# A hand-ordered plan for retention attention and a SoLU layer on one core: small column work in pairs, half states copied on three engines, eight chunks with the plain output weight, and a new order of all steps

## The chip, the cores and the metric

The kernel runs on one core of one Trainium2 chip. The metric is the device time of one execution in microseconds (us). Beside the plain runs there is one profiled execution, whose trace gives the start and the length of every instruction on TensorE (PE, with its weight loads as PEld), VectorE (DVE), ScalarE (ACT), GpSimd (POOL) and of every transfer that SyncE (SP) issues. Times inside the trace are counted from its first instruction.

## The reference, cut to what matters

Eight sequences of 576 rows pass through retention with eight heads of 64 columns; the joined heads (512 columns) pass through a wide layer with a softmax gate and a layer norm, and through an output weight.

```python
# q, k, v: (8, 8, 576, 64); w_in: (512, 1024); w_out: (1024, 512); g_ln: (1024,); all float32
gamma = 1.0 - 2.0 ** (-5.0 - np.arange(H))
Dmat = np.where(rel >= 0, gamma[:, None, None] ** rel[None], 0.0)   # rel = row - column
ret = (q @ k.transpose(0, 1, 3, 2) / np.sqrt(64)) * Dmat @ v
x = ret.transpose(0, 2, 1, 3).reshape(8 * 576, 512)
h = x @ w_in
e = np.exp(h - h.max(-1, keepdims=True))
solu = h * e / (e.sum(-1, keepdims=True) + 1e-9)
mu = solu.mean(-1, keepdims=True)
var = ((solu - mu) ** 2).mean(-1, keepdims=True)
out = ((solu - mu) / np.sqrt(var + 1e-6) * g_ln) @ w_out
```

## The kernel before, in words

**Chunks.** Each sequence has four chunks of 128 rows and a tail of 64; the tails of two sequences share one chunk. That makes 36 chunks. Two sequences alternate, so chunks 0, 2, 4 and 6 are the first sequence, 1, 3, 5 and 7 the second, and 8 their common tail; then the next two sequences follow. Retention is done chunk by chunk: scores inside the chunk, and a running state (one 64 by 64 block for each head) that carries all earlier chunks of the sequence.

**One chunk, step by step.** `lq`, `lk`, `lv` (lines 151 to 160) load the rows of q, k and v, 256 KB each, into rings of eight buffers. `q`, `k`, `v` (lines 171 to 180) cast them to 16 bits, q and v with a factor for each row and head. `TL:a.b` (line 188) is one group of transposes on TensorE: q and k of chunk a, and the gated rows u of an older chunk b; `eX` and `eY` (lines 224 to 229) copy its two halves out of PSUM. `sc` (line 234) makes the scores, `m0` (line 255) multiplies the decay mask in, `kp` (line 266) makes the chunk's part of the state, `t` (line 308) adds it to the old state, `s16` (line 318) makes the 16-bit copy of the new state, as two instructions for the two halves of the partitions, and `s32` (line 325) the decayed float copy. `xs` and `xv` (lines 278 and 294) add what the old state and the chunk itself give to the same PSUM bank, `xT` (line 333) copies the sum out. `mm1` (line 351) is the product with w_in, 16 matmuls of 512 columns; `max`, `exp`, `solu`, `sq` (lines 369, 379, 408 and 427) are the row maximum, the exponential with its row sum, the gate product with its row sum, and the sum of squared deviations. `w1`, `w2` and `pow` (lines 401, 434 and 441) make the row's factor from these sums, one column of 128 values at a time. `mm2` (line 479) is the product with the output weight, `osb` (line 498) multiplies the row factor while copying out of PSUM, `st` (line 509) stores 128 rows of the result.

**The output weight.** The mean over the 1024 gated columns must be taken out. Two ways are used. For chunks below `RAW`, 5 before, `uc` (line 415) subtracts the mean from the gated rows, and `mm2` uses `w_raw16`, the weight times g_ln, which `ws` (line 543) makes. For the other chunks the mean is taken out of the weight: `mean` (line 558) is a matmul of ones with `w_raw16`, `evm` copies its result out, and `cw` (line 570) subtracts it, eight blocks into `w_out16`. So `mean` needs all eight `ws`, and these need the four loads `wo` of w_out. In the same way the first `mm1` needs the four loads `wi` of w_in and the casts `cwA` and `cwB`.

**The order.** Nothing is scheduled by a planner at run time. `PLAN` (lines 584 to 681) is one list of words, followed from left to right (`follow`, line 684): `name:chunk@engine/banks`, with v for VectorE, s for ScalarE and g for GpSimd. Each engine does its own steps in the order of the list, and so does SP's queue of transfers, where loads and stores stand in one row. A step that waits holds up all later steps of its engine. `warm:k` (line 577) is k matmuls on zeros whose result nobody reads. The order of the transfers in the old list is:

```
wi:0 lk:0 lq:0 lq:1 lk:1 wi:1 lv:0 wi:2 wi:3 lv:1 lq:3 lk:3 lq:2 lk:2 lv:3 lv:2 lq:4 lk:4 lq:5 lk:5 lk:6
lv:4 lv:5 lq:6 lv:6 wo:2 wo:0 wo:3 wo:1 lq:7 lq:8 lk:7 lk:8 lv:7 lq:9 lk:9 lq:10 lk:10 st:0 lv:8 lv:9
lq:11 st:1 lv:10 lk:11 lv:11 st:3 lq:12 lk:13 lv:13 lq:13 lk:12 lq:15 lq:14 lk:14 lk:15 lv:12 lv:15 st:2
lk:17 st:4 lq:17 st:7 lk:19 st:5 lv:17 lv:16 lk:16 lv:14 st:6 lq:16 lv:18 lv:19 st:8 lq:18 st:9 st:10 lk:18
lq:19 lq:22 lq:20 st:11 lv:23 lv:21 lv:20 lk:21 lq:26 lk:20 lq:21 lq:24 lk:22 lk:26 st:12 lv:26 lq:23 lk:23
lk:24 lq:25 lv:22 st:14 st:13 lk:27 lv:28 lk:25 st:15 lv:27 lq:27 lq:28 lv:24 lv:25 st:16 lq:35 lk:29 lk:28
lq:29 st:18 st:17 lv:30 lk:30 lv:29 lk:32 st:19 lk:34 lq:30 lk:33 lk:35 lq:32 st:20 st:22 lv:34 lq:31 lk:31
lq:33 st:21 lv:35 lq:34 lv:31 lv:33 lv:32 st:25 st:24 st:23 st:26 st:27 st:28 ...
```

## Time and profile before

| what | value |
|---|---|
| three runs | 220.24, 222.17 and 223.47 us, median 222.17 us |
| the profiled execution, its own time | 222.2 us |
| its span, first to last instruction | 220.5 us |
| TensorE clock granted, mean | 0.994 |
| moved by DMA | 42.51 MB, 193 GB/s over the span |
| read from and written to HBM | 32.53 MB and 9.44 MB |

The profile's page gives busy time for each engine, the same in forty slices, the transfers, and groups of like instructions with their count, mean length and the idle time before them. The share of a whole span hides that the start, the middle and the end have different limits, so the prediction goes by stretches of time. The lost time that it speaks of is, at a point of the trace, the time on the clock less the time that TensorE had spent on work that the result needs; `warm` matmuls count as lost.

### The profile page before, as it was taken

How to read it: one execution, taken by the hardware profiler on the slowest of the kernel's cores; microseconds unless marked ns; L12 is line 12 of the kernel's file. 1: busy time of each engine (PE TensorE's matmuls, PEld its weight loads, DVE VectorE, ACT ScalarE, POOL GpSimd, SP SyncE). 2: the span in 40 equal slices, each digit the busy share in tenths (PEclk: the TensorE clock that was granted, in tenths of full speed). 3: DMA queues.
4: the chain of work that ended last, by engine and by line, in shares of the span. 5: the costliest groups of instructions: out<-in, count | busy, mean ns of one | idle time of the engine just before them, and what ended most of it. 6: DMA issues, size and time to landing. Idle time of an engine off the chain costs nothing. (4 is left out here: it accounts for less than half of the span.)

```text
span 220.5 us, 8347 instructions
## 1 busy us (share of the span) xinstructions
PE 203.5 (92%) x3486; PEld 122.2 (55%) x3486; DVE 192.2 (87%) x316; ACT 169.3 (77%) x273; POOL 160.5 (73%) x270
## 2 busy tenths in 40 slices
...
DMA  6999999997999989999998997899889920310224
GB/s 160 264 310 195 225 205 299 253 204 166 205 262 190 187 234 250 239 281 222 201 226 204 251 253 170 206 240 221 183 209 212 193 103 0 98 52 4 95 98 143
DMA packets 120806, 42.51 MB, mean 193 GB/s; under 512 B 114496, under 2 KB 114752, under 8 KB 120768
## 3 DMA queue, kind: packets, MB, share of 16 engines
q1 hardware_dynamic: 119728, 41.98, 82.8%
...
q14 instruction: 11, 0.09, 0.2%
HBM read 32.53 MB, written 9.44 MB: 190 GB/s over the span
## 5 line engine op out<-in xcount | busy, mean ns | idle before, releaser
L341 PE MATMUL ps<-w_in,xT 128*64 128x512 f16 x576 | 68.3, 381 | 0.3 <-DVE tt L132 0.2
L341 PE MATMUL ps<-w_out,tt 128*64 128x512 f16 x480 | 56.3, 380 | 0.0
L409 DVE SCALAR_TENSOR_TENSOR u<-ps,e 128x1024 f16<-128x1024 f32 (+1 forms) x37 | 43.7, 1188 | 4.2 <-ACT e L380 3.8
L370 DVE TENSOR_REDUCE col_nm<-ps 128x1 f32<-128x1024 f32 (+1 forms) x37 | 43.9, 1188 | 3.9 <-PE ps L341 3.2
L380 ACT ACTIVATE e<-ps,col_nm 128x1024 f32<-128x1024 f32 (+1 forms) x37 | 40.5, 1096 | 8.1 <-DVE col_nm L370 7.2
L130 ACT COPY tt<-ps 128x1024 f16<-128x1024 f16 (+1 forms) x46 | 42.4, 960 | 5.1 <-PE ps L207 4.4
L247 DVE TENSOR_TENSOR ret<-ps,masks 128x1024 f16<-128x1024 f32 x36 | 43.5, 1216 | 2.9 <-PE ps L240 1.9
L341 PEld LDWEIGHTS <-xT 128*64 128x64 f16 x576 | 31.1, 110 | 25.8 <-ACT xT L130 1.0
L341 PEld LDWEIGHTS <-tt 128*64 128x64 f16 x560 | 31.1, 110 | 24.0 <-issue 0.4
L428 ACT ACTIVATE e<-u,col_su 128x1024 f32<-128x1024 f16 (+1 forms) x37 | 41.8, 1132 | 1.6 <-DVE u L409 1.6
L166 POOL TENSOR_TENSOR q<-qf,small 128x512 f16<-128x512 f32 x33 | 34.5, 1049 | 1.7 <-DMA qf<-in_q_dram 1.4
L166 POOL TENSOR_TENSOR v<-vf,small 128x512 f16<-128x512 f32 x31 | 32.8, 1061 | 2.0 <-DMA vf<-in_v_dram 1.8
L130 ACT CAST xT<-ps 128x512 f16<-128x512 f32 x33 | 19.3, 585 | 12.1 <-PE ps L300 8.8
L322 POOL CAST s<-t 64x256 f16<-64x256 f32 x64 | 26.6, 416 | 2.2 <-DVE col_nmu L416 0.2
L442 POOL TENSOR_TENSOR col_rs<-col_w,mhalf 128x1 f32<-128x1 f32 x36 | 21.2, 592 | 8.2 <-DVE col_w L435 7.9
L506 ACT ACTIVATE o_sb<-ps,col_rs 128x512 f32<-128x512 f32 x30 | 20.5, 691 | 6.2 <-POOL col_rs L442 5.0
L132 POOL CAST k<-kf 128x512 f16<-128x512 f32 x30 | 19.1, 642 | 7.9 <-DMA kf<-in_k_dram 7.6
L132 DVE COPY tt<-ps 128x1024 f16<-128x1024 f16 (+1 forms) x32 | 19.4, 615 | 3.5 <-PE ps L207 3.5
L579 PE MATMUL ps<-zeros 128*128 128x512 f16 x62 | 18.1, 428 | 1.2 <-DVE zeros L698 1.2
L402 POOL TENSOR_SCALAR col_w<-col_s 128x1 f32<-128x1 f32 x36 | 11.0, 309 | 10.6 <-ACT e L380 10.2
L327 POOL TENSOR_TENSOR s<-t,small 128x256 f32<-128x256 f32 x24 | 14.8, 618 | 4.8 <-DVE t L313 4.1
L207 PE MATMUL ps<-ident,q 64*128 64x64 f16 x288 | 11.0, 191 | 6.4 <-DVE u L409 2.1
...
## 6 DMA issues: line engine op xcount, KB each, us to landing
kf<-in_k_dram SPq DMA_DIRECT2D x32, 256.0 KB, 5.1
qf<-in_q_dram SPq DMA_DIRECT2D x32, 256.0 KB, 5.2
vf<-in_v_dram SPq DMA_DIRECT2D x32, 256.0 KB, 4.9
out_dram<-o_sb SPq DMA_DIRECT2D x32, 256.0 KB, 3.4
w_in<-in_moe_w_in_dram SPq DMA_DIRECT2D x4, 512.0 KB, 5.6
w_out<-in_moe_w_out_dram SPq DMA_DIRECT2D x4, 512.0 KB, 7.0
...
```

The costliest lines, as they stand in the source:

```text
L130: nc.scalar.copy(out=out, in_=in_)
L132: {"v": nc.vector, "g": nc.gpsimd}[eng].tensor_copy(out=out, in_=in_)
L166: {"v": nc.vector, "g": nc.gpsimd}[eng].tensor_tensor(out=out, in0=in_, in1=table.unsqueeze(2).to_broadcast([P, H, D]), op=ALU.mult)
L247: nc.vector.tensor_tensor(out=ret[n % RB][:, 4 * e : 4 * e + w].rearrange("p a b -> p (a b)"), in0=bank(b0, w * P), in1=masks[:, 1 if is_t ...
L322: nc.gpsimd.tensor_copy(out=st16[b % 2][c % 2][ee, :, e], in_=T_OF[n][ee])
L341: nc.tensor.matmul(out=o[ee], lhsT=lhs(ee), rhs=rhs, start=start, stop=stop)
L370: nc.vector.tensor_reduce(out=col("nm", n, j), in_=h(n, j), axis=AX.X, op=ALU.max, negate=True)
L380: nc.scalar.activation(out=e_[n % EB][:, part(j)], in_=h(n, j), func=ACT.Exp, bias=col("nm", n), accum_out=col("s", n, j),)
L409: nc.vector.scalar_tensor_tensor(out=u_[n % UB][:, part(j)], in0=h(n, j), scalar=1.0, in1=e_[n % EB][:, part(j)], op0=ALU.mult, op1=ALU.mu ...
L428: nc.scalar.activation(out=e_[n % EB][:, part(j)], in_=u_[n % UB][:, part(j)], func=ACT.Square, bias=col("su", n), scale=-1.0 * DFF, accum ...
L442: nc.gpsimd.tensor_tensor(out=col("rs", n), in0=col("w2", n), in1=mhalf, op=ALU.pow)
L506: nc.scalar.activation(out=dst, in_=o, func=ACT.Copy, scale=col("rs", n))
```

## The change

The change leaves the arithmetic as it is, apart from what runs where and when.

- `w1`, `w2` and `pow` handle the columns of two chunks, 2k and 2k+1, in one instruction (`pair`), 19 times each where there were 36; only chunks 34 and 35 are done alone. `w1` moves from GpSimd to VectorE. The row factor of the first chunk of a pair is now there only when the sums of the second are.
- `s16` is one half of the partitions at a time, each with its own engine: 26 halves on GpSimd, 24 on ScalarE, 14 on VectorE, where GpSimd did all 64.
- `RAW` is 8, so eight chunks go through `uc` and `w_raw16`, and `w_out16` is first needed by chunk 9. Of the eight `uc` steps five are on GpSimd and three on VectorE (five on VectorE before); of the eight `cw` steps five are on GpSimd, as two instructions each, and three on VectorE (all on VectorE before).
- `PLAN` is a new order of all steps. Some casts and copies change engines in it: `k` has 23 on GpSimd, 12 on ScalarE and 1 on VectorE (30, 6 and 0 before), `v` 35 on GpSimd and 1 on VectorE (31 and 5). `warm` has 57 matmuls (62 before). The other steps have the same number as before.
- The new names `ut_` and `dT` are not used: the ring has length 0 and the plan holds no `dT`.

The order of the transfers in the new list, to its end:

```
lq:0 lk:1 wi:0 lv:0 lk:0 lq:2 lq:1 lv:1 wi:3 lk:2 wi:1 wi:2 lq:4 lk:3 lv:2 lq:5 lq:3 lv:4 lk:4 lk:5 lv:3
lk:6 wo:3 lq:6 wo:2 wo:0 lv:5 wo:1 lv:6 lk:7 lq:7 lv:7 lq:9 lq:8 lk:8 lk:9 lq:10 lk:11 lv:8 lk:14 lk:10
lq:11 lv:9 lv:10 st:0 st:3 lq:12 st:1 lq:13 lk:12 lv:13 lk:13 lv:11 st:2 lq:14 lv:15 lv:12 lq:15 lk:17 st:6
st:4 lk:15 st:5 lq:16 lk:16 st:7 lv:14 lv:19 lq:17 lv:16 lk:20 lk:18 lq:19 st:9 st:8 lv:17 lk:19 lq:18 lv:18
lv:20 lk:23 lq:20 lk:22 lk:21 lq:22 lq:25 st:10 lv:21 lq:21 lk:26 st:11 lq:23 lk:25 st:14 lv:22 lq:24 lk:24
lq:27 st:12 lv:24 st:15 lq:26 lk:27 st:13 lk:29 lv:23 lv:29 lk:28 lk:33 st:16 lq:30 lq:29 lv:25 st:17 lq:35
lv:28 st:18 lv:27 st:19 lk:30 lk:35 lv:26 lq:28 lq:32 st:20 lk:31 lv:32 lq:31 lv:31 lv:33 st:21 lq:34 lv:30
lq:33 st:23 lk:32 lk:34 st:22 lv:35 lv:34 st:26 st:27 st:25 st:24 st:29 st:28 ...
```

The diff, with the plan cut to the start and the places that the prediction speaks of:

```diff
--- before.py
+++ after.py
@@ -75,7 +75,7 @@
         return chunks[n][1] == 4
 
 
-    LB, QB, KB, TB, RB, XB, EB, UB, UCB, OB, TQ = 8, 4, 6, 5, 3, 3, 3, 3, 2, 4, 2
+    LB, QB, KB, TB, RB, XB, EB, UB, UCB, OB, TQ, UTB = 8, 4, 6, 5, 3, 3, 3, 3, 2, 4, 2, 0
 
     def ring(count, shape, dtype, name):
         return [const.tile([P] + shape, dtype, name=f"{name}{i}") for i in range(count)]
@@ -86,7 +86,7 @@
     ident = const.tile([P, P], F16, name="ident")
     ones = const.tile([P, P], F16, name="ones")
     zeros = const.tile([P, 512], F16, name="zeros")
-    mhalf = const.tile([P, 1], FP, name="mhalf")
+    mhalf = const.tile([P, 2], FP, name="mhalf")
     gln = const.tile([P, NF], FP, name="gln")
     g32 = const.tile([P, NF], FP, name="g32")
     w_in32 = const.tile([P, 4, DFF], FP, name="w_in32")
@@ -107,6 +107,7 @@
     e_ = ring(EB, [DFF], FP, "e")
     u_ = ring(UB, [DFF], F16, "u")
     uc_ = ring(UCB, [DFF], F16, "uc")
+    ut_ = ring(UTB, [8, P], F16, "ut")
     o_sb = ring(OB, [DM], FP, "o_sb")
     cols = {}
 
@@ -317,9 +318,8 @@
     @step
     def s16(n, j, eng, bk):
         (b,), c = chunks[n]
-        for e in range(2):
-            ee = slice(64 * e, 64 * e + 64)
-            nc.gpsimd.tensor_copy(out=st16[b % 2][c % 2][ee, :, e], in_=T_OF[n][ee])
+        ee = slice(64 * j, 64 * j + 64)
+        copy(eng, st16[b % 2][c % 2][ee, :, j], T_OF[n][ee])
 
     @step
     def s32(n, j, eng, bk):
@@ -397,10 +397,15 @@
     def ssadd(n, j, eng, bk):
         add(nc.vector, "ss", n)
 
+
+    def pair(name, n):
+        return cols[name][:, n : n + (2 if n < NCH - 2 else 1)]
+
     @step
     def w1(n, j, eng, bk):
-        nc.gpsimd.tensor_scalar(
-            out=col("w1", n), in0=col("s", n), scalar1=col("s", n), scalar2=1e-6 * DFF,
+        col("w1", n)
+        nc.vector.scalar_tensor_tensor(
+            out=pair("w1", n), in0=pair("s", n), scalar=1e-6 * DFF, in1=pair("s", n),
             op0=ALU.mult, op1=ALU.mult,
         )
 
@@ -413,6 +418,16 @@
 
     @step
     def uc(n, j, eng, bk):
+        if eng == "g":
+            nc.gpsimd.tensor_scalar(
+                out=col("nmu", n), in0=col("su", n), scalar1=-1.0 / DFF, scalar2=0.0, op0=ALU.mult,
+                op1=ALU.add,
+            )
+            nc.gpsimd.tensor_scalar(
+                out=uc_[n % UCB], in0=u_[n % UB], scalar1=1.0, scalar2=col("nmu", n), op0=ALU.mult,
+                op1=ALU.add,
+            )
+            return
         nc.vector.tensor_scalar(
             out=col("nmu", n), in0=col("su", n), scalar1=-1.0 / DFF, scalar2=None, op0=ALU.mult,
             op1=ALU.bypass,
@@ -432,14 +447,19 @@
 
     @step
     def w2(n, j, eng, bk):
+        col("w2", n)
         nc.vector.scalar_tensor_tensor(
-            out=col("w2", n), in0=col("ss", n), scalar=1.0 / DFF**2, in1=col("w1", n),
+            out=pair("w2", n), in0=pair("ss", n), scalar=1.0 / DFF**2, in1=pair("w1", n),
             op0=ALU.mult, op1=ALU.add,
         )
 
     @step
     def pow_(n, j, eng, bk):
-        nc.gpsimd.tensor_tensor(out=col("rs", n), in0=col("w2", n), in1=mhalf, op=ALU.pow)
+        col("rs", n)
+        w = pair("w2", n)
+        nc.gpsimd.tensor_tensor(
+            out=pair("rs", n), in0=w, in1=mhalf[:, 0 : w.shape[1]], op=ALU.pow
+        )
 
     def lp_src(n, c):
         return u_[n % UB][:, c * P : (c + 1) * P]
@@ -480,14 +500,25 @@
         WHERE["o", n, j] = bk[0]
         w = DM if j is None else DM // 2
         a = 0 if j is None else j * w
-        t = tt[TL_OF["u", n]]
-        t = t if j is not None else t[:, 8:16]
+        if n in DT:
+            t = ut_[DT.index(n) % UTB]
+        else:
+            t = tt[TL_OF["u", n]]
+            t = t if j is not None else t[:, 8:16]
         wt = w_raw16 if n < RAW else w_out16
         for c in range(NF):
             wide_mm(
                 bank(bk[0], w), lambda m: t[:, c, m], wt[:, c, a : a + w],
                 c == 0, c == NF - 1,
             )
+
+
+    DT = []
+
+    @step
+    def dT(n, j, eng, bk):
+        src = uc_[n % UCB] if n < RAW else u_[n % UB]
+        nc.sync.dma_start(out=ut_[DT.index(n) % UTB], in_=src, transpose=True)
 
     def o_part(n, j):
         w = DM if j is None else DM // 2
@@ -568,6 +599,12 @@
 
     @step
     def cw(c, j, eng, bk):
+        if eng == "g":
+            w = w_out32[:, c]
+            gc = g32[:, c : c + 1].to_broadcast([P, DM])
+            nc.gpsimd.tensor_tensor(out=w, in0=w, in1=gc, op=ALU.mult)
+            nc.gpsimd.tensor_tensor(out=w_out16[:, c], in0=w, in1=mean_sb, op=ALU.subtract)
+            return
         nc.vector.scalar_tensor_tensor(
             out=w_out16[:, c], in0=w_out32[:, c], scalar=g32[:, c : c + 1], in1=mean_sb,
             op0=ALU.mult, op1=ALU.subtract,
@@ -582,104 +619,107 @@
 
 
     PLAN = """
...
+        lq:0 warm:30/7 lk:1 wi:0 lv:0 lk:0 lq:2 lq:1 k:1@g lv:1 wi:3 v:0@v q:0@v lk:2 k:0@v
+        TL:0./140 wi:1 kp:0/5 eY:0.@s warm:3/7 t:0 eX:0.@v wi:2 sc:0/01 q:1@v warm:2/7 q:2@v
+        TL:1./261 warm:5/7 lq:4 eY:1.@s v:1@g m0:0 eX:1.@s cwA:0@g s16:0.0@v lk:3 sc:1/01
+        s16:0.1@g kp:1/4 m0:1 warm:4/7 lv:2 k:2@s t:1 xv:1/6 cwB:3@s cwB:0@v TL:2./352 s32:1
+        xT:1@s warm:2/7 lq:5 cwA:1@v cwA:3@g s16:1.0@s xv:0/6 eX:2.@s warm:2/7 eY:2.@v cwB:1@g
+        sc:2/34 warm:2/7 lq:3 cwA:2@v cwB:2@s m0:2 mm1:1/01 lv:4 q:4@g xT:0@v lk:4 k:3@s
+        mm1:0/56 max:1 s16:1.1@s lk:5 v:2@g exp:1 xs:2/4 max:0 s32:0 xv:2/4 lv:3 warm:3/7
+        xT:2@s g32 q:5@g solu:1 exp:0 mm1:2/23 lk:6 q:3@g sq:1 solu:0 wo:3 v:4@g TL:3./713
+        warm:3/0 eX:3.@s eY:3.@v lq:6 uc:0@g max:2 k:4@s xs:3/4 sc:3/01 sq:0 kp:2/6 wo:2 m0:3
+        k:5@g TL:4.0/754 exp:2 uc:1@g t:2 wo:0 eX:4.0@v eY:4.0@s v:3@g solu:2 TL:5.1/160 lv:5
+        warm:1/0 eX:5.1@s s32:2 xv:3/4 eY:5.1@v sc:4/23 uc:2@g xT:3@s wo:1 kp:3/7 m0:4 sc:5/01
+        ws:7@s mm1:3/45 k:6@s lv:6 q:6@g t:3 s16:2.1@s m0:5 s16:3.0@s s16:2.0@s s32:3 ws:6@s
+        lk:7 xs:4/3 max:3 kp:4/7 ws:4@g xv:4/3 ws:5@s TL:6.2/601 xT:4@s t:4 lq:7 ws:1@g exp:3
+        eX:6.2@v mm1:4/23 ws:0@v s32:4 lv:7 eY:6.2@s solu:3 v:5@g s16:4.0@s sc:6/67 s16:3.1@s
+        lq:9 ws:3@g s16:4.1@v ws:2@s xv:5/5 max:4 xs:6/4 xs:5/5 kp:5/0 xT:5@s mean/1 lq:8
+        v:6@g m0:6 exp:4 uc:3@g lk:8 w1:0 w1:2 k:7@s t:5 xv:6/4 solu:4 kp:6/7 evm mm1:5/56
+        lk:9 q:7@g xT:6@s sq:3 uc:4@v lq:10 v:7@g t:6 TL:7.3/432 sq:2 mm1:6/01 eX:7.3@v
...
+        lq:18 m0:16 eY:17.13@s mm1:15/34 s16:14.0@g lv:18 s32:14 xT:14@s lv:20 s16:14.1@v
+        v:17@g t:15 sq:12 t:16 lk:23 sc:17/67 max:15 v:19@g lq:20 mm1:14/12 s16:16.0@s
+        s16:15.0@s m0:17 lk:22 exp:15 q:18@g xv:16/0 xs:16/0 max:14 mm2:10/5 k:19@g s16:16.1@s
+        lk:21 xT:16@s v:18@g s16:15.1@s solu:15 exp:14 lq:22 xs:17/6 xv:17/6 kp:19/7 w1:10
+        kp:18/0 xT:17@s TL:19.15/344 t:19 lq:25 k:23@g t:18 sq:15 mm1:16/67 solu:14 eX:19.15@s
...
+        s16:21.0@g lk:33 s16:21.1@v exp:21 m0:22 mm1:20/34 osb:16@s solu:21 eX:23.19@s v:23@g
...
+        s16:24.0@s osb:20@s st:20 xv:27/7 q:28@g max:25 sc:26/56 lk:31 xs:26/4 mm2:21/3 lv:32
+        v:26@g m0:26 lq:31 exp:25 lv:31 w1:22 lv:33 xv:26/4 solu:25 TL:28.24/263 xT:26@s
...
+        osb:33@s st:34 mm2:35.0/6 st:33 osb:35.1@s st:35.1 osb:35.0@v st:35.0
     """
-    RAW = 5
+    RAW = 8
```

169 lines of the change are left out of this document (73 added, 96 removed).

## The prediction

> **What bounds the kernel now.** I read the page first: the shares of the engines, and the slices of the transfers.
>
> ```profile
> span 220.5 us, 8347 instructions
> PE 203.5 (92%) x3486; PEld 122.2 (55%) x3486; DVE 192.2 (87%) x316; ACT 169.3 (77%) x273; POOL 160.5 (73%) x270
> ...
> DMA  6999999997999989999998997899889920310224
> ...
> q1 hardware_dynamic: 119728, 41.98, 82.8%
> ...
> kf<-in_k_dram SPq DMA_DIRECT2D x32, 256.0 KB, 5.1
> ...
> w_in<-in_moe_w_in_dram SPq DMA_DIRECT2D x4, 512.0 KB, 5.6
> ```
>
> PE leads, but the transfers are at 8 or 9 tenths in nearly every slice until about 175 us. Then the windows; the second fence is the same table for the `warm` line alone.
>
> ```profile
> 10.00:40.00 30.00, 27.52 (x449) 14.71 (x451) 24.89 (x39) 19.28 (x32) 24.26 (x36) 1.00 1.08 254
> 40.00:70.00 30.00, 27.70 (x480) 16.81 (x478) 29.17 (x42) 25.36 (x39) 27.93 (x39) 1.00 0.97 204
> 70.00:103.50 33.50, 32.81 (x613) 20.49 (x609) 31.53 (x51) 29.73 (x47) 30.93 (x55) 1.00 1.02 237
> 103.50:129.70 26.20, 24.53 (x520) 15.65 (x516) 23.33 (x35) 23.59 (x37) 20.25 (x31) 1.00 1.04 222
> 129.70:160.00 30.30, 27.41 (x491) 17.06 (x492) 26.64 (x42) 22.40 (x38) 23.79 (x42) 1.00 0.92 211
> 160.00:203.80 43.80, 43.20 (x764) 27.29 (x758) 42.14 (x64) 36.91 (x61) 28.44 (x54) 1.00 0.45 109
> ```
>
> ```profile
> 10.00:40.00 30.00, 9.64 (x35) 2.60 (x35) 1.00 1.08 254
> ```
>
> The first number after each length is PE's busy time. PE loses 30 - 27.52 + 9.64 = 12.1 us from 10 to 40, then 2.3, 0.7, 1.7, 2.9 and 0.6 us. DVE is at 97% from 40 to 70 and the limit there. From 103 to 160 no engine is: 4.6 us go although DVE has 6.5 idle. The waits of that stretch (108 to 160) and the casts that end them tell why.
>
> ```profile
> POOL k L132 <- DMA kf<-in_k_dram: 6.7, 4, 3.5
> ...
> ACT k L130 <- DMA kf<-in_k_dram: 2.6, 1, 2.6
> ```
>
> ```profile
> 19.70 0.61 POOL L132 CAST k<-kf 128x512 f16<-128x512 f32 x1 [0.60 <-DMA kf<-in_k_dram]
> ...
> 70.16 1.05 POOL L166 TENSOR_TENSOR q<-qf,small 128x512 f16<-128x512 f32 x1 [0.59 <-DMA qf<-in_q_dram]
> ...
> 110.62 0.61 POOL L132 CAST k<-kf 128x512 f16<-128x512 f32 x1 [3.45 <-DMA kf<-in_k_dram]
> ...
> 132.91 0.61 POOL L132 CAST k<-kf 128x512 f16<-128x512 f32 x1 [1.42 <-DMA kf<-in_k_dram]
> ...
> 154.61 0.62 ACT L130 CAST k<-kf 128x512 f16<-128x512 f32 x1 [2.61 <-DMA kf<-in_k_dram]
> ```
>
> By the order of the list these are `k:3`, `q:13`, `k:21`, `k:25` and `k:32`. I count the queue in units of 256 KB: a load or store of 128 rows is one, the two halves of a joined tail together one, a `wi` or `wo` two. Their places are units 16, 59, 94, 112 and 129, so one unit takes 1.23, 1.19, 1.18, 1.19 and 1.20 us, counted from the start of the trace. The queue runs as one straight line of 1.19 us a unit, whatever the engines do. It is the second limit beside PE, and each cast in the list has an earliest time: its unit times 1.19.
>
> **The change, part by part.** First the engines, with these groups.
>
> ```profile
> L322 POOL CAST s<-t 64x256 f16<-64x256 f32 x64 | 26.6, 416 | 2.2 <-DVE col_nmu L416 0.2
> ...
> L442 POOL TENSOR_TENSOR col_rs<-col_w,mhalf 128x1 f32<-128x1 f32 x36 | 21.2, 592 | 8.2 <-DVE col_w L435 7.9
> ...
> L402 POOL TENSOR_SCALAR col_w<-col_s 128x1 f32<-128x1 f32 x36 | 11.0, 309 | 10.6 <-ACT e L380 10.2
> ...
> L435 DVE SCALAR_TENSOR_TENSOR col_w<-col_ss,col_w 128x1 f32<-128x1 f32 x36 | 8.3, 241 | 0.3
> ...
> L571 DVE SCALAR_TENSOR_TENSOR w_out<-w_out,g,mean_sb 128x512 f16<-128x512 f32 x8 | 7.0, 908 | 0.0
> ...
> L420 DVE TENSOR_SCALAR uc<-u,col_nmu 128x1024 f16<-128x1024 f16 x5 | 4.2, 833 | 0.2
> ...
> L130 ACT COPY tt_last<-ps 128x256 f16<-128x256 f16 x2 | 0.8, 400 | 0.0
> ...
> L132 DVE COPY tt_last<-ps 128x256 f16<-128x256 f16 x2 | 0.6, 278 | 0.0
> ```
>
> POOL loses 38 halves at 0.416 (15.8 us), 17 `pow` at 0.592 (10.1) and all 36 `w1` at 0.309 (11.1): -37.0. It gains ten `cw` instructions of the shape of its q cast, 1.05 each (10.5); five `uc`, each a column at 0.31 and 1024 elements at between two casts (1.2) and two products (2.1), say 1.4, as it has one tensor in (8.6); net four `v` and minus seven `k` (about 0). Net about -18 of 160. DVE loses five `cw` (4.5), 17 `w2` (4.1), two `uc` (1.7) and four `v`; it gains 19 `w1` at `w2`'s 0.241 (4.6) and 14 halves. A half on DVE or ACT has no row; nearest are the copies of 256 columns, 0.28 and 0.40. From below the 0.24 of one column bounds both; from above, a DVE instruction between two SBUF tiles can stretch, as `uc` did:
>
> ```profile
> L420 DVE TENSOR_SCALAR uc<-u,col_nmu x5: 497/642/1351, 27.0 to 49.6; 128x1024 f16<-128x1024 f16 x5
> ```
>
> So up to 0.28 + 0.85. I take the copies, which have the same 256 columns: +3.9 on DVE (3.4 to 15.8), 24 x 0.40 = 9.6 on ACT (5.8 to 9.6), which also gets six `k` at 0.62 (3.7). DVE comes out some 4 down, ACT some 12 up to 181 of 220. None of this is on PE's path outside 40 to 70, where DVE is relieved (the first `w_out16` product is chunk 9's now, so `cw` is due later as well); ACT's additions are covered by its 51 us of idle time, and without that each half costs its 0.40.
>
> The pair adds a wait: `osb` of an even chunk now waits for `sq` of the next. The list puts both `sq` ahead of each `pow`, so I cost it at nothing; behind it stand the store and, in SP's queue, the loads after that store (a rival below). `k:3` on ACT waits for unit 18, 21.4 us; `exp:1` behind it needs the maximum of the first `mm1`, due at about 22.7, so that wait is covered. PE's work is unchanged; five `warm` fewer only make room.
>
> Then the moved loads, which decide. For PE's work left after a step I use the chain of waits.
>
> ```profile
> 190.50 1.85 PE ps L341 x16
> ...
> 192.80 0.12 PE ps L270 x8
> ...
> 193.58 0.47 PE ps L207 x32
> ...
> 195.89 0.22 PE ps L300 x8
> 196.12 0.33 PE ps L240 x8
> ...
> 204.81 0.57 PE ps L207 x32
> ...
> 210.16 0.23 PE ps L455 x16
> ```
>
> A wide product is 1.85, `kp` 0.12, `xv` and `xs` 0.22, `sc` 0.33, half a `TL` 0.25; the whole list (70 wide products, four halves, the mean at 1.9, 36 `sc`, 64 `xv` and `xs`, 32 `kp`, 71 halves of `TL`) comes to 183. Four gates of the new order, each at its unit times 1.19:
>
> Start: `wi:2` is unit 16 (19.0 us; `wi:3` was unit 13), so the first `mm1` slips by nearly 4 us, but two then run in a row. The mean needs `wo:1`, unit 36 (42.8) and a `ws` of 1.05: 43.9 us, with 17.2 us of useful PE work before it, so 26.7 lost. Before it began here:
>
> ```profile
> 45.15 1.92 PE L341 MATMUL ps<-w_raw,ones 128*64 128x512 f16 x16
> ```
>
> with 21.2 of work done, 24.0 lost. The start is 2.7 worse. `kp:18` needs `lv:18`, unit 87 (103.5) and the cast 1.05: 104.6, then 43 wide products (79.6), four halves (3.8), 18 `sc`, 32 `xv` and `xs`, 15 `kp`, 39 halves of `TL`, `lp`: 108.1. `xv:23` needs unit 114 (135.7): 136.8, then 76.4. `xv:26` is the last: `lq:28`, unit 131 (29 + 28 + 27 full loads, 18 stores, 26 half units, 16 for the weights), lands at 155.9, and on POOL `v:26` stands behind `q:28`: two casts of 1.05, so 158.1. After it come 22 wide products (40.7), four halves (3.8), 8 `sc` (2.6), 16 `xv` and `xs` (3.5), 8 `kp` (1.0), 19 halves of `TL` (4.8), `lp` 0.2: 56.6. PE's end to the span's end, the last `osb` and store, was 4.8. Gates in us of span: 217.5, 218.0, and 158.1 + 56.6 + 4.8 = 219.5.
>
> The same sum for the old list: `kp:31` waits for `v:31`, which POOL casts at 175.05:
>
> ```profile
> 175.05 1.04 POOL L166 TENSOR_TENSOR v<-vf,small 128x512 f16<-128x512 f32 x1
> ...
> 213.80 1.91 PE L341 MATMUL ps<-w_out,tt_last 128*64 128x256 f16 x32
> ```
>
> 176.1 + 38.7 + 4.8 = 219.6 against the 220.5 measured. So the method is 0.9 short, and I add 0.6 to the new 219.5 (there is less after its gate to go wrong on DVE): span 220.1. What the start loses and what DVE saves from 40 to 70 both vanish in this gate. The profiled execution's own time, 222.2, is 1.7 over its span and equal to the median of 222.17; so 220.1 gives 221.8.
>
> A rule speaks against the line of 1.19. The Trainium skill, "DMA: Bandwidth & Descriptors", section "Why small descriptors are slow (HBM only)", gives a 256-byte descriptor 11 cycles where 8 carry data; with the 435 GB/s that this page's section "Where 436 GB/s comes from" states, that is 316 GB/s, an estimate of 0.83 us a unit, and unit 131 would land at 109 us. The trace has 1.19, so the measurement decides; by the page no load would be a gate, which is the first rival.
>
> **The rivals.** (1) The loads are no gate: the straight line was the engines' pace and not the queue's. For it: DMA's share reaches 1.08 in the windows, so 1.0 need not be full. Against it: the line holds at 19.7 us as at 154.6. Then there remain the start's 26.7 lost and, with DVE relieved, some 0.8 of the old 2.3 from 40 to 70: 183 + 27.5 + 4.8 = 215.3 of span, 217.0.
>
> (2) Slower: SP's queue stands at stores. `st:0` to `st:8` stand close behind their `osb`, and every load behind a store waits with it.
>
> ```profile
> SPq L513 <- ACT o_sb L506: 37.4, 14, 10.7
> ```
>
> It decides where SP stands longer than a transfer is under way (5.1 us, the `kf` row): only then does the line bend. Two such stands of 3 us beyond that, ahead of `lq:28`, give 226.1 of span, 227.8. Against it: these waits have not bent the line before.
>
> (3) Also slower: the three `uc` on POOL in the first 35 us, and the casts behind them, cost 2.1 each or more, and POOL, not the loads, is late at `q:28`. It decides when POOL is over 155.9 there; 116 us of work stand before it, so 37 us are spare. About 3 us late: 225.
>
> (4) The pairing does nothing for the time, as POOL is idle 27%: that is in the forecast.
>
> **How the numbers follow.** Forecast 0.62 (221.8, its own range 219.5 to 224: one per cent in the rate moves unit 131 by 1.6 us, and up to 1 us of new stalls), rival 1 0.16, rival 2 0.13, rival 3 0.09. The range over them is 217.0 to 226.0. About 2% is what a measurement here tells from no change: below 217.7 lie most of rival 1, 0.12; above 226.6 most of rival 2 and a third of rival 3, 0.16; within, 0.72.
>
> **What would show it.** Right: the casts that wait for DMA stand on 1.19 us a unit (`v:18` near 103.5, `q:28` near 156); `xv:26` starts near 158; the mean near 44; POOL's busy time near 143, ACT's near 181. Wrong: POOL never waits for loads after 70 us and `xv:26` comes before 154 (rival 1); SP's queue idle for over 5 us ahead of a store before 150 us (rival 2); POOL busy without gaps up to `q:28` (rival 3).

## The result and the profile after

The changed kernel took 232.25 us in the median of four runs (227.98 to 234.24), the kernel before 222.06 us beside it. The ratio of the two is 1.037 with a 95% interval of 1.029 to 1.045: slower. Like every ratio below, it is made from undisturbed runs alone, and so it can differ from the ratio of the medians. The forecast was 221.8 us with a range up to 226.0. The profiled execution was the shortest of the four, 227.98 us with a span of 226.3.

From the page of the changed kernel, the same lines as in the prediction, and the slices of the clock:

```profile
span 226.3 us, 8276 instructions
...
PE 205.4 (91%) x3481; PEld 122.9 (54%) x3481; DVE 199.9 (88%) x324; ACT 178.0 (79%) x299; POOL 144.6 (64%) x196
...
PEclk9999997999999999999999999999999999999998
DMA  7999999999999698989999989879999413011034
...
q1 hardware_dynamic: 119728, 41.98, 80.2%
```

GpSimd and ScalarE came out as forecast (144.6 and 178.0 for 143 and 181). VectorE did not: 199.9 for 188, and 192.2 before. Its work grew where it was to shrink. The clock has a dent near 33 us that the kernel before had not.

The windows of the changed kernel, with the edges of the prediction's table (the first number after each length is PE's busy time, the third DVE's):

```profile
10.00:40.00 30.00, 27.23 (x418) 14.41 (x419) 25.08 (x39) 20.87 (x38) 20.69 (x28) 0.94 1.09 266
40.00:70.00 30.00, 28.32 (x508) 18.07 (x506) 29.72 (x48) 28.04 (x47) 26.56 (x30) 1.00 1.00 209
70.00:103.50 33.50, 31.39 (x588) 20.29 (x586) 33.23 (x45) 30.00 (x51) 30.42 (x39) 1.00 0.90 209
103.50:129.70 26.20, 23.28 (x412) 13.54 (x408) 23.53 (x37) 22.29 (x38) 18.21 (x25) 1.00 1.00 219
129.70:160.00 30.30, 28.99 (x554) 18.18 (x548) 27.52 (x41) 25.41 (x41) 19.15 (x29) 1.00 0.93 211
160.00:203.80 43.80, 39.64 (x748) 24.58 (x746) 41.98 (x65) 35.55 (x58) 24.68 (x34) 1.00 0.52 124
```

Up to 70 us PE is busy for nearly as long in both kernels. It loses more in three later stretches: PE idles 2.1 us from 70 to 103.5 (0.7 before), 2.9 from 103.5 to 129.7 (1.7), and 4.2 from 160 to 203.8 (0.6); from 129.7 to 160 it is the other way, 1.3 for 2.9. VectorE is idle for 0.6 us out of 63.5 from 40 to 103.5, where the prediction had relieved it.

The casts of the gates, from GpSimd's timeline of the changed kernel: by the order of the list they are `v:18`, `v:23`, and `q:28` with `v:26` behind it. The second fence has PE's `xv:26`.

```profile
105.64 1.04 POOL L167 TENSOR_TENSOR v<-vf,small 128x512 f16<-128x512 f32 x1 [0.51 <-DMA vf<-in_v_dram]
...
137.86 1.04 POOL L167 TENSOR_TENSOR v<-vf,small 128x512 f16<-128x512 f32 x1 [3.47 <-DMA vf<-in_v_dram]
...
160.01 1.04 POOL L167 TENSOR_TENSOR q<-qf,small 128x512 f16<-128x512 f32 x1 [3.51 <-DMA qf<-in_q_dram]
161.01 1.04 POOL L167 TENSOR_TENSOR v<-vf,small 128x512 f16<-128x512 f32 x1
```

```profile
162.11 0.41 PE L301 MATMUL ps<-ret,v 128*64 128x128 f16 x8 [1.10 <-POOL v L167]
```

The loads of the first three were to land at 103.5, 135.7 and 155.9. They are units 87, 114 and 131, so a unit takes 1.214, 1.209 and 1.221 us instead of 1.19. The list's gate is where the prediction put it, and 4.1 us late. A candidate for what bent the line is in the waits of SP's queue between 45 and 160 us, first of the kernel before, then of the changed one:

```profile
SPq L513 <- ACT o_sb L506: 8.6, 7, 2.7
```

```profile
SPq L544 <- ACT o_sb L537: 15.9, 12, 2.5
```

Twelve stands of at most 2.5 us at stores whose `osb` is not done, 15.9 us in all, with the loads behind them.

The second cause is among the groups and the line of the copies (the three numbers behind `x14` in the second fence are the shortest, the median and the longest of one, in ns):

```profile
L133 DVE CAST s<-t 64x256 f16<-64x256 f32 x14 | 9.8, 700 | 0.3
...
L407 DVE SCALAR_TENSOR_TENSOR col_w<-col_s 128x2 f32<-128x2 f32 x17 | 6.2, 372 | 0.0
L451 DVE SCALAR_TENSOR_TENSOR col_w<-col_ss,col_w 128x2 f32<-128x2 f32 x17 | 4.7, 284 | 0.2
L608 DVE SCALAR_TENSOR_TENSOR w_out<-w_out,g,mean_sb 128x512 f16<-128x512 f32 x3 | 3.5, 1178 | 0.0
```

```profile
L133 DVE CAST s<-t x14: 275/502/2562, 15.0 to 207.1; 64x256 f16<-64x256 f32 x14
```

A half on VectorE takes 0.275 us at best, as forecast, and 2.56 us at worst. The worst one in the timelines of VectorE, GpSimd and PE:

```profile
187.73 2.56 DVE L133 CAST s<-t 64x256 f16<-64x256 f32 x1
190.33 1.23 DVE L414 SCALAR_TENSOR_TENSOR u<-ps,e 128x1024 f16<-128x1024 f32 x1
```

```profile
187.10 3.04 POOL L167 TENSOR_TENSOR v<-vf,small 128x512 f16<-128x512 f32 x3
```

```profile
191.61 0.32 PE L271 MATMUL ps<-v,k 128*64 128x64 f16 x8 [2.23 <-DVE u L414]
```

The half ends with GpSimd's third cast in a row, the gate product behind it is late, and PE stands 2.23 us. The Trainium skill's page "SBUF — State Buffer", section "SBUF: two separate sides", gives a shared pair of SBUF ports, for a whole instruction, to whichever starts first of a GpSimd instruction and a VectorE instruction of certain kinds, and has the other fully blocked. The trace fits that, except that here the half ended not with one cast but with the third in a row; that the ports are the reason is argued, not shown.

### The profile page after: what moved, and what is told of

It is laid out like the page before. It is cut to its first block, busy times and chain, and to the rows that moved or that the text cites. A ratio compares the mean times of both kernels' runs of the same rounds, so it can differ in the third digit from the quotient of the medians.

```text
span 226.3 us, 8276 instructions
## 1 busy us (share of the span) xinstructions
PE 205.4 (91%) x3481; PEld 122.9 (54%) x3481; DVE 199.9 (88%) x324; ACT 178.0 (79%) x299; POOL 144.6 (64%) x196
## 4 chain that ended last, share of the span: by engine, by line
PE 31%; DVE 20%; POOL 15%; DMA 11%; SPq 8%; issue 6%; ACT 5%; DVEq 0%; POOLq 0%
PE ps L341 24%; SPq L147 6%; DMA qf<-in_q_dram 5%; POOL v L167 5%; DVE u L414 4%; DVE ret L248 4%; DVE col_nm L370 4%; DMA w_in<-in_moe_w_in_dram 3%; PE ps L208 3%; POOL q L167 3%; DMA vf<-in_v_dram 3%; DVE s L133 2%; POOL w_out L606 2%; PE ps L301 2%; POOL uc L426 1%
## 5 line engine op out<-in xcount | busy, mean ns | idle before, releaser
L341 PE MATMUL ps<-w_out,tt 128*64 128x512 f16 x432 | 50.9, 381 | 0.0
L341 PEld LDWEIGHTS <-xT 128*64 128x64 f16 x576 | 33.6, 111 | 28.5 <-issue 4.0
L167 POOL TENSOR_TENSOR v<-vf,small 128x512 f16<-128x512 f32 x35 | 38.0, 1093 | 17.3 <-DMA vf<-in_v_dram 15.2
L380 ACT ACTIVATE e<-ps,col_nm 128x1024 f32<-128x1024 f32 (+1 forms) x37 | 40.4, 1092 | 10.9 <-DVE col_nm L370 10.4
L370 DVE TENSOR_REDUCE col_nm<-ps 128x1 f32<-128x1024 f32 (+1 forms) x37 | 43.9, 1189 | 4.5 <-PE ps L341 4.2
L167 POOL TENSOR_TENSOR q<-qf,small 128x512 f16<-128x512 f32 x32 | 33.2, 1042 | 8.9 <-DMA qf<-in_q_dram 8.8
L460 POOL TENSOR_TENSOR col_rs<-col_w,mhalf 128x2 f32<-128x2 f32 (+1 forms) x19 | 12.9, 684 | 24.7 <-DVE col_w L451 24.5
L537 ACT ACTIVATE o_sb<-ps,col_rs 128x512 f32<-128x512 f32 (+1 forms) x29 | 19.6, 680 | 1.3 <-POOL col_rs L460 0.8
L616 PE MATMUL ps<-zeros 128*128 128x512 f16 x57 | 16.5, 430 | 1.2 <-DVE zeros L738 1.2
L133 POOL CAST k<-kf 128x512 f16<-128x512 f32 x23 | 14.2, 621 | 4.6 <-DMA kf<-in_k_dram 3.5
L133 POOL CAST s<-t 64x256 f16<-64x256 f32 x26 | 10.4, 400 | 10.5 <-PE ps L301 5.6
L301 PE MATMUL ps<-ret,v 128*64 128x128 f16 x288 | 14.3, 220 | 3.1 <-POOL v L167 1.4
L301 PEld LDWEIGHTS <-v 128*64 128x64 f16 x288 | 11.3, 110 | 8.5 <-issue 3.4
```

The lines of the kernel that those rows point to most:

```text
L133: {"v": nc.vector, "g": nc.gpsimd}[eng].tensor_copy(out=out, in_=in_)
L167: {"v": nc.vector, "g": nc.gpsimd}[eng].tensor_tensor(out=out, in0=in_, in1=table.unsqueeze(2).to_broadcast([P, H, D]), op=ALU.mult)
L301: nc.tensor.matmul(out=o, lhsT=v16[n % KB][:, 2 * hp + e], rhs=ret[n % RB][:, 4 * e + hp], start=first and hp == 0, stop=True, skip_group_ ...
L341: nc.tensor.matmul(out=o[ee], lhsT=lhs(ee), rhs=rhs, start=start, stop=stop)
L370: nc.vector.tensor_reduce(out=col("nm", n, j), in_=h(n, j), axis=AX.X, op=ALU.max, negate=True)
L380: nc.scalar.activation(out=e_[n % EB][:, part(j)], in_=h(n, j), func=ACT.Exp, bias=col("nm", n), accum_out=col("s", n, j),)
```

## The experiments

Each kernel differs from the changed one or from the one before as its diff shows; all were timed in at least six runs against the kernel before, whose median stayed between 221.67 and 222.47 us. Two theories were put against each other, and against a third, the clock:

- A: loads come late because stores stand ahead of them in SP's queue;
- B: state halves on VectorE are stretched beside GpSimd's work, and what waits for VectorE is late;
- C: PE is busy for too little of some stretch in the first 40 us, and gets half its clock behind it.

### One cause at a time

**Stores later.** The words `st:0` to `st:27` moved down the list.

```diff
-    ... osb:0@s solu:7 xv:8/3 osb:1@s sc:9/01 st:0 TL:10.6/270 st:3 ...
+    ... (each st:n, n up to 27, 24 words further on)
```

> The changed kernel with each store of chunks 0 to 27 set 24 words later in the list, everything else in its place. If the loads come late because SP's queue stands at stores (about 20.7 us of stands ahead of lq:28), the stands shrink to a few us, v:18 lands near 103.5 instead of 105.6, q:28 near 156 instead of 159.9, and the profiled span falls by 3 to 4 us to 222.5 to 223.5. If the halves on VectorE or the clock carry the loss, the loads come earlier and the span stays within 1 us of 226.3, since the casts or the PE are late next. The half-clock stretch near 33 us should stay in either case, as nothing before 48 us moves.

Measured: 231.11 us, ratio 1.033 (1.025 to 1.041), span 225.7. The loads moved, the time hardly. `v:18` and `q:28` no longer wait for their loads (by the order of the list their casts begin at 102.17 and 157.06 us, for 105.64 and 160.01), and still PE stands longer just before `v:18`. The row of SP's stands at `osb` falls from 15.9 to 9.8 us, but all rows of SP at the stores' line together only from 23.0 to 22.4, so how late the loads come can't be read from the sum of the stands. From the timeline of this kernel, all engines:

```profile
98.50 3.24 DVE L133 CAST s<-t 64x256 f16<-64x256 f32 x1
...
98.54 2.03 POOL L167 TENSOR_TENSOR v<-vf,small 128x512 f16<-128x512 f32 x2
...
100.54 1.03 POOL L167 TENSOR_TENSOR q<-qf,small 128x512 f16<-128x512 f32 x1
...
102.24 1.92 PE L341 MATMUL ps<-w_in,xT 128*64 128x512 f16 x16 [2.61 <-DVE t L316]
```

With the loads there, GpSimd casts three times in a row, VectorE's half lasts from 98.50 to 101.74, `t` is late, and PE idles 2.61 us. A alone is not the whole cause.

**Halves off VectorE.**

```diff
-    s16:0.0@v ... s16:4.1@v ... s16:33.1@v          (14 words)
+    s16:0.0@s ... s16:4.1@s ... s16:33.1@s
```

> The changed kernel with the 14 state halves that VectorE copies put on ScalarE at the same places of the list. If the halves on VectorE are a cause (9.8 us of its time, one of 2.56 us at 187.7 on the chain of waits), DVE falls from 199.9 to about 190, ACT rises by 14 x 0.40 = 5.6 us to about 184, and the span falls by 2 to 4 us. If only the loads and the clock count, the span stays within 1 us of 226.3: the 187.7 stall goes, but what stands behind it was late anyway. If ScalarE is as tight, xT and the evictions come later and the span grows by up to 3 us.

Measured: 229.46 us, ratio 1.032 (1.025 to 1.038). VectorE fell to 189.9 us as expected, the median by 2.8 (by the ratios, 1.037 and 1.032, about 1 us). Now PE stands for a late load. From the timeline of this kernel at 152 us:

```profile
152.48 1.04 POOL L167 TENSOR_TENSOR v<-vf,small 128x512 f16<-128x512 f32 x1 [2.17 <-DMA vf<-in_v_dram]
...
153.59 0.40 POOL L133 CAST s<-t 64x256 f16<-64x256 f32 x1
...
154.01 0.42 DVE L316 TENSOR_TENSOR t<-ps,s 128x256 f32<-128x256 f32 x1 [2.91 <-POOL s L133]
...
154.49 1.92 PE L341 MATMUL ps<-w_in,xT 128*64 128x512 f16 x8 [2.80 <-DVE t L316]
```

A cast on GpSimd waits 2.17 us for its load; a half of the state stands behind it in GpSimd's queue; `t` of the next chunk needs the half's source buffer (there are two); PE needs the bank that `t` reads. A late load stops PE over four engines, 2.80 us. The halves spread over the engines are what ties the state chain to GpSimd's waiting casts. B alone is not the whole cause either.

**More dummy products.**

```diff
-    warm:1/0
+    warm:6/0
```

> The changed kernel with one dummy step made larger, warm:1/0 at about 32 us becomes warm:6/0, 5 more dummy products of 0.21 us each. If the halved clock at 33.3 to 36.7 us comes from too thin a PE in the 3.4 us before it, the stretch goes, the profiled run gains 1.7 us there less up to 1.05 us for the dummies (span 225.5 to 226.5), and the median of the runs, whose clocks were 0.967 to 0.988, comes down from 232 towards 228. If the clock is not set there, the stretch stays and the span grows by 0 to 1 us; the median stays near 232.

Measured: 233.74 us, ratio 1.056 (1.050 to 1.061). The half-clock stretch at 33 us went, and two others came, at 111 and 196 us. Windows of 3.41 us of this kernel, the second and the fourth those at half clock:

```profile
107.60:111.01 3.41, 1.59 (x52) 1.21 (x54) 1.82 (x4) 2.41 (x6) 2.31 (x4) 1.00 0.95 208
111.01:114.42 3.41, 3.41 (x42) 1.60 (x40) 1.92 (x5) 1.90 (x3) 2.34 (x4) 0.50 1.16 225
192.93:196.34 3.41, 1.12 (x34) 0.72 (x32) 3.38 (x5) 1.25 (x3) 1.22 (x2) 1.00 0.37 140
196.34:199.75 3.41, 3.41 (x72) 2.64 (x68) 3.12 (x7) 2.31 (x4) 1.55 (x4) 0.50 0.06 21
```

Both follow a window in which PE was busy for less than half the time. So it is not the place near 33 us alone that decides: where PE stands, the price can be paid again, and 3.41 us at half speed cost up to 1.7 us of work. This was a miss: all six runs took 233.09 to 235.57 us, and by the ratio (1.056 for 1.037) the kernel got slower. The span grew by 5.5 us (231.8 for 226.3). Two half-clock stretches for one (1.7 us) and five dummies at the expectation's 0.21 explain 2.8 of them; the rest is not explained.

### Causes together

**All three edits.**

> The three edits together in the changed kernel: stores 24 words later, five more dummy products, the 14 halves on ScalarE. If these three are the whole of the loss against the kernel before (38.1 us of PE time lost against 32.3), the span comes to about 219 to 221, the time to 220.5 to 223. If the new order itself or the pairing costs the rest, it stays at 223 or more.

Measured: 222.16 us (221.13 to 223.84 in twelve runs), ratio 1.003 (1.000 to 1.007), span 220.2: level with the kernel before. The page's clock line is at 9 in all slices, and `q:28`, unit 130 here, comes on the old line (153.76 / 130 = 1.183):

```profile
153.76 1.04 POOL L167 TENSOR_TENSOR q<-qf,small 128x512 f16<-128x512 f32 x1 [1.08 <-DMA qf<-in_q_dram]
```

**Without the dummy products.**

> The changed kernel with the stores 24 words later and the 14 halves of VectorE on ScalarE, without the extra dummy products. Theory: late loads and halves stretched on VectorE each leave gaps of 2 to 3 us in the PE, either alone is enough to lose the time, and a thin stretch of the PE is followed by 3.41 us at half clock. Then this kernel is close to all three together: profiled span 219.5 to 221.5, and only the thin place near 30 us may still give one half-clock stretch in some runs (1.2 us), median 222 to 224. Rival: the dummy products near 32 us were what brought the clock to 1.0; then half-clock stretches appear here in most runs and the median is 226 or more.

Measured: 222.69 us, ratio 1.003 (0.999 to 1.007). Beside the other two edits the dummy products do not matter, so C is no cause of its own. Stores and halves alone are worth 9.6 us together by the medians, and 1.1 and 2.8 apart; by the ratios (1.037 for the changed kernel, then 1.003, 1.033 and 1.032) it is 7.4 us together and about 1 us each.

The lost time (start of a step less the useful work before it, at the prices of the prediction) in the profiled executions, in us:

| useful work done | before | changed | stores later | halves off | all three |
|---|---|---|---|---|---|
| 20 | 24.0 | 25.5 | 24.7 | 24.7 | 26.0 |
| 80 | 28.0 | 32.0 | 32.6 | 32.6 | 29.7 |
| 120 | 31.2 | 34.5 | 35.0 | 38.4 | 30.7 |
| 160 | 33.2 | 38.2 | 37.6 | 38.9 | 31.0 |
| last `mm2` | 32.3 | 38.1 | 37.5 | 40.0 | 32.1 |

With stores later or halves off alone the loss only changes its place; with all three edits it is gone. What all three have over the kernel before from 20 to 160 (5.0 us lost for 9.2) is what the change brings without its two faults; its start, 2.0 us worse, and its end take it back.

### One part in the old order

**Halves on three engines**, each on the engine that the change gives it, nothing else.

```diff
-    s16:0 ... s16:1 ...
+    s16:0.0@v s16:0.1@g ... s16:1.0@s s16:1.1@s ...
```

> The kernel before with one part of the change alone: each state copy split into its two halves on the engines that the change gives them (26 on GpSimd, 24 on ScalarE, 14 on VectorE), at the old places of the list. If the halves on VectorE cost time in any order, its halves take 0.5 to 3 us beside GpSimd's casts, the state chain is late in places, and the time grows by 1 to 4 us over 222.2 with some half-clock stretches. If only the new order brings it out, the time is within 0.5 us of before, or 1 us better from the 20 us taken off GpSimd.

Measured: 232.05 us, ratio 1.046 (1.040 to 1.052), at a clock of 0.999 in the profiled run. This part alone, in the old order, costs as much as the whole change, and its trace has no half-clock stretch before PE's end.

**The same without VectorE** (the 14 words `@v` as `@s`).

> The kernel before with its state halves on two engines, 26 on GpSimd and 38 on ScalarE, none on VectorE, at the old places. The same split with 14 of them on VectorE took 232.05 us at an undisturbed clock (0.999). If VectorE is the engine that the middle of the list waits for (it was busy 205.2 us there, 192.2 before), taking 9.4 us off it again brings the time back to 221 to 224. If the splitting itself or ScalarE's halves (9.6 us, then 15.2) cost the time, it stays at 227 or more.

Measured: 225.25 us, ratio 1.014 (1.008 to 1.020). The 9.6 us over the kernel before (232.05 for 222.47) became 3.6 (225.25 for 221.67): about 6 come with VectorE's halves. The rest I put down to the split itself with ScalarE's halves, in places that were chosen for GpSimd; no run takes these apart.

**The same with VectorE's halves from PSUM.** A half is then the sum that `t` forms, over 64 partitions, right behind `t`.

```diff
-        copy(eng, st16[b % 2][c % 2][ee, :, j], T_OF[n][ee])
+        o = st16[b % 2][c % 2][ee, :, j]
+        if eng != "v":
+            return copy(eng, o, T_OF[n][ee])
+        kpp = bank(WHERE["kp", n], 256).rearrange("p (a b) -> p a b", a=4)[ee]
+        if c == 0:
+            nc.vector.tensor_copy(out=o, in_=kpp)
+        else:
+            nc.vector.tensor_tensor(out=o, in0=kpp, in1=st32[b % 2][(c - 1) % 2][ee], op=ALU.add)
```

> The kernel before with its halves on three engines, but each of VectorE's 14 made from the bank in PSUM (the same sum that step t forms, over 64 partitions) right behind t, instead of from the copy in SBUF. The SBUF form took 0.27 to 3 us a half and the time 232.05; without VectorE's halves it was 225.25. If VectorE's SBUF-only copies are stretched by what GpSimd does at the time, the PSUM form takes 0.3 to 0.45 us every time, VectorE falls by 4 us or more from 205 and the time comes to 225 to 228. If it is only that VectorE has 14 more things to do and each delays the next, it stays at 230 or more.

Measured: 229.11 us, ratio 1.036 (1.026 to 1.046): between the two answers. VectorE's busy time fell from 205.2 to 200.0 us. The PSUM form gives back 2.5 of the 6 us, so in the old order VectorE's load as such, or the place, counts for more than the stretch. The stretch was smaller there than in the new order, too: the SBUF form in the old order has no half of "3 us", as the expectation says, but one of 1.50 at most.

```profile
L132 DVE CAST s<-t x14: 274/470/1498, 16.7 to 208.4; 64x256 f16<-64x256 f32 x14
```

**In the new order, with later stores.**

> The changed kernel with the stores 24 words later and VectorE's 14 halves made from PSUM right behind t. With the SBUF halves on VectorE it took 231.11, with them on ScalarE 222.69. If the stretch of the SBUF form is the cause, no half is longer than 0.5 us, the 2 to 3 us gaps of the PE near 99 and 189 us go, and the time comes to 222 to 225. If VectorE's load as such is, it is 227 or more.

Measured: 222.82 us, ratio 1.005 (1.001 to 1.010), where the SBUF form took 231.11 with the same stores. The line of the ten halves that are sums:

```profile
L329 DVE TENSOR_TENSOR s<-ps,s x10: 405/427/429, 40.4 to 198.8; 64x256 f16<-64x256 f32 x10
```

None is over 0.43 us. Engine and count are the same, the source is another, and so is the place, right behind `t`. So here VectorE's load as such was not the cause; the stretch was, or the place, which no run takes apart. It also shows that ten VectorE instructions with one source in PSUM and one in SBUF were not stretched.

**On GpSimd instead** (the 14 words `@g`, stores later).

> The changed kernel with the stores 24 words later and VectorE's 14 halves put on GpSimd instead of ScalarE: GpSimd gains 14 x 0.40 = 5.6 us to about 150, its casts and halves queue a little longer. If only freeing VectorE counts, the time is 222 to 224 as with ScalarE; if halves that stand behind waiting casts in GpSimd's queue hold the state chain, it is 225 or more.

Measured: 222.09 us, ratio 1.002 (0.997 to 1.007). Freeing VectorE is enough, wherever the halves go.

**Pairing alone**, chunks 0 to 31, each pair at the place of its later chunk.

> The kernel before with pairing alone for chunks 0 to 31: one instruction for two chunks' columns, the first product on VectorE instead of GpSimd, both set at the place of the later chunk. VectorE gains 16 x 0.26 and loses 16 x 0.24 us, so nothing; GpSimd loses 16 x 0.55 + 32 x 0.31 less 16 x 0.15, some 16 us. If GpSimd's small work and its stands counted before, the time falls by 0.5 to 2 us; if pairing makes the row factors late enough to hold the stores and the loads behind them, it grows by 1 to 3 us; if neither, it is within 0.5 us of before.

Measured: 226.94 us in the median of twelve runs that reach from 222.04 to 228.47, nine of them at 225.78 or more; ratio 1.006 (0.998 to 1.013). Unclear: the steps' places had to be set anew, and these may be what it shows.

### What the other parts are worth once the two causes are gone

**One chunk at a time** in the kernel with all three edits: two instructions wherever `pair` did one, at the same places.

> All three edits, and the small column work done for one chunk at a time, at the places of the paired steps: 17 more instructions each for the two products on VectorE and for the power on GpSimd. If pairing is worth what it removes, VectorE gains 17 x (0.1 to 0.3) x 2 = 4 to 10 us of work and GpSimd 17 x 0.55 = 9 us, and the time grows by 0.5 to 3 us against 222.2. If it lies beside other work, the time stays within 0.5 us of 222.2.

Measured: 224.44 us, ratio 1.011 (1.005 to 1.017). The pair is worth about 2 us.

**`uc` and `cw` back on VectorE** (`@g` as `@v` in ten words, five of each; the expectation counted nine).

> All three edits, and the four weight pieces and five centred copies that GpSimd does put back on VectorE: VectorE gains about 4 x 0.9 + 5 x 0.9 = 8 us, GpSimd loses about 4 x 2.4 + 5 x 1.3 = 16 us. If GpSimd's new work was a cause (casts queue behind it), the time falls by 1 to 2 us below 222.2, mostly before 75 us. If VectorE bounds the start, it grows by 1 to 4 us.

Measured: 226.57 us, ratio 1.022 (1.017 to 1.027). GpSimd's share is worth about 4 us.

**All of `uc` and `cw` on GpSimd** (`@v` as `@g` in the other six).

> All three edits, and the three weight pieces and three centred copies that VectorE still does on GpSimd too: VectorE loses 3.2 + 2.4 = 5.6 us, GpSimd gains 3 x 2.4 + 3 x 1.3 = 11 us, all before 75 us. The reverse move (9 pieces on VectorE, 8 us) cost 4.4 us, so if VectorE is what counts, this gains 1 to 2.5 us, to 220 to 221. If GpSimd's casts then come late at 45 to 75 us, it loses 1 to 2 us instead.

Measured: 230.90 us, ratio 1.040 (1.034 to 1.045). A miss: VectorE lost 3.5 us of work and the time grew by 8.7. The share that the change chose lies between two slopes. Why the second is so steep is not shown.

**`w1` on GpSimd again.**

> All three edits, and the first of the two small products on GpSimd again, one chunk at a time, as in the kernel before: VectorE loses 17 instructions of 0.26 us, 4.4 us, GpSimd gains 36 of 0.31 us, 11 us, and waits at each for the exponential's sum. If only VectorE's load counts, the time falls by 1 to 2 us; if GpSimd's waits hold the casts behind them, it grows by 0.5 to 2 us.

Measured: 224.53 us, ratio 1.012 (1.009 to 1.016). VectorE got 1.4 us lighter, and it cost about 2.

### Looking for a version that beats both

**The kernel before with later stores.**

> The kernel before with each store of chunks 0 to 27 set 24 words later and nothing else. SP stood at its stores for about 8.8 us before 155 us. If loads are a gate in the old order too, the loads come up to 2 us earlier and the time falls by 1 to 2 us to 220 to 221; if they lie ahead of their casts there, the time is within 0.5 us of 221.7 to 222.5; if the o_sb buffers come free too late, it grows.

Measured: 221.23 us, ratio 0.996 (0.992 to 1.000). At most 0.8% faster, and not surely so. The loads did come earlier: `k:32`, whose cast waited 2.61 us for its load at 154.61 in the kernel before, is cast at 150.81 without a wait. So the loads were not the only gate of the old order. A new wait took the place of some of what they held, as ScalarE's timeline has it:

```profile
172.65 0.69 ACT L506 ACTIVATE o_sb<-ps,col_rs 128x512 f32<-128x512 f32 x1 [2.55 <-POOL v L166]
```

The releaser named is wrong: by the order of the list this is `osb:25`, which needs the buffer of `st:21`, and that store landed at 172.5 us.

**With a fifth `o_sb` buffer** (`OB` 5), in the old order and in the best mixture of the new one.

> The kernel before with the stores of chunks 0 to 27 24 words later and a fifth output buffer o_sb. With four buffers the later stores moved the wait: at 170.1 us ScalarE stood 2.55 us at an o_sb step while a store was still on its way, and the PE stood 2.47 us behind it. If the buffer was the cause, that stand goes and the time falls from 221.2 by 1.5 to 2.5 us to 218.5 to 220. If GpSimd's row factor was late, it stays at 221.

> The changed kernel with what the runs have shown: stores 24 words later, a fifth o_sb buffer, warm:6/0, and VectorE's 14 halves put on ScalarE up to chunk 10 (where GpSimd waits for w_out) and on GpSimd after it. The two forms apart took 222.1 to 222.7, with half-clock stretches before 45 us in the one and a loss of 3.8 us after 60 us in the other. If those losses add up, it takes 219 to 221. If the start of the new order (2 us later at the mean than the old one) and VectorE bound it, it stays at 222.

Measured: 225.04 us, ratio 1.019 (1.012 to 1.026), and 223.40 us, ratio 1.010 (1.004 to 1.016). Both worse than with four buffers. ScalarE in the first of them:

```profile
80.58 0.69 ACT L506 ACTIVATE o_sb<-ps,col_rs 128x512 f32<-128x512 f32 x1 [6.11 <-DMA out_dram<-o_sb]
```

That is `osb:7`. Buffers go by chunk number, and with five of them chunk 7 has chunk 2's, whose store, 24 words later, landed at 80.5; with four it had chunk 3's. So the fifth buffer made a new wait of 6.11 us (2.51 in the other kernel). Buffers given out in the order of `osb` were not tried, and no version that is clearly faster than the kernel before was found.

## Why the prediction was wrong, point by point

**The line of the loads: wrong.** The step "the queue runs as one straight line of 1.19 us a unit, whatever the engines do" failed. The new list puts stores where their `osb` is late, and the loads behind them came 2 us late at unit 87 and 4 at unit 131; in the kernel with all three edits they were on the line again, at 1.183 us a unit. The second rival named this, but with a wrong point of decision: it asked for stands longer than a transfer's 5.1 us, and the twelve at `osb` were of 2.5 us at most, 15.9 in all against 8.6 before. That its 227.8 us lies beside the profiled 227.98 is luck, since late loads are not the whole of the loss. Nor did the trial of the sum on the old list test the line: the prediction's own row of `v:31` at 175.05 shows no wait for a load, and PE did not wait for `v:31` either, as its row of `kp:31` in the kernel before shows none:

```profile
176.63 0.29 PE L270 MATMUL ps<-v,k 128*64 128x64 f16 x8
```

**The price of the halves: wrong, and the largest fault.** "I take the copies": 3.9 us for 14 halves, measured 9.8. The bounds (3.4 to 15.8) held the sum, but the step that followed, "none of this is on PE's path outside 40 to 70", did not hold. The bound came from `uc`, stretched by at most 0.85 us; a half was stretched by 2.29 (2.56 less 0.275) and in another run by 2.96. A stretch some ten times as long as the instruction counts like a wait, and it stood in front of the gate product (`solu`). VectorE, forecast 4 us lighter, became 7.7 heavier; of the 11.7 between, 5.9 are the halves and 2.7 the paired `w1` and `w2` (10.9 us for 34 of them, taken at 0.241); the other 3.1 are not broken down.

**The gate and the work after it: the mechanism was right in part, the size was not.** `xv:26` began at 162.11 us behind `q:28` and `v:26`, 4.0 late. From there to the end of the span it took 64.2 us for 61.4 forecast (56.6 and 4.8); the 2.23 us behind the stretched half are most of that. With the 0.6 that the prediction added, these two (4.0 and 2.8) are the 6.2 us by which the span missed 220.1. The gate was not the load's alone: with later stores `q:28` did not wait, and `xv:26` still began at 161.33.

**The dummy products: the step was incomplete.** "Five `warm` fewer only make room" held for the time beside the other two edits, as the runs with and without five more agree (222.16 and 222.69); in the changed kernel itself five more made it slower. The step left out the clock. The windows of the changed kernel ahead of the dent and in it:

```profile
29.87:33.28 3.41, 2.19 (x69) 1.40 (x61) 3.41 (x6) 3.40 (x7) 3.31 (x6) 1.00 1.04 262
33.28:36.69 3.41, 3.41 (x34) 1.71 (x30) 2.83 (x4) 3.37 (x8) 3.14 (x5) 0.50 0.99 309
```

A window in which PE was busy 2.19 us was followed by one at half clock. No term of the sum had a price for that. How little is too little is not a simple threshold: a later window of the same trace, with PE busy for less, was followed by the full clock.

```profile
104.96:108.37 3.41, 1.94 (x56) 1.43 (x58) 1.83 (x4) 2.75 (x6) 1.83 (x3) 1.00 0.90 200
108.37:111.78 3.41, 3.41 (x60) 1.68 (x54) 3.22 (x7) 3.24 (x5) 2.30 (x4) 1.00 1.23 240
```

**The start: right in size.** By the order of the list the mean began at 42.7 us with 25.4 lost, for 43.9 and 26.7 forecast.

**`uc`, `cw` and GpSimd: right.** A `uc` on GpSimd took 1.31 us (0.19 and 1.12) for 1.71 taken (0.31 and 1.4), `cw` 1.04 and 1.34 for 1.05 each; GpSimd's total was off by 1.6 us. The third rival did not come; moving this work either way costs 2 to 4%. (The spare time given there, 155.9 less 116, is 39.9 us and not 37.)

**The pair at nothing: wrong in the other direction.** As said, it held up hardly any `osb`; ScalarE's wait for the row factor fell from 5.0 us in all to one of 0.8:

```profile
ACT o_sb L506 <- POOL col_rs L442: 5.0, 4, 2.0
```

```profile
ACT o_sb L537 <- POOL col_rs L460: 0.8, 1, 0.8
```

One instruction for two chunks is worth about 2 us once the two faults are gone. The prediction looked for its worth on GpSimd, which had time.

**Why it was wrong by ten us and not by four.** The prediction's sum over gates takes the last gate alone, and would have put late loads at 4 us. The profiled execution, the shortest of the four, is only 5.9 us above the kernel before. The other three took 230.76, 233.73 and 234.24 us at clocks of 0.981, 0.967 and 0.968, where the profiled one had 0.988. An estimate: 0.02 of its span of 226.3 us is 4.5 us, so most of what they took longer goes with the clock, for which the sum had no term. And the two faults hide each other: where one is undone, PE stands for the other, as the columns of lost time show, so undoing one gives 1 to 3 us back by the medians and undoing both 9.6. The sum also has no term for an engine as full as VectorE (0.99 of the stretches from 40 to 103.5 us), which has no idle time left to take up a delay; that this passes delays on is argued, not shown.

What stays open: how much of the halves' cost in the new order is the stretch and how much the place, why the split of the halves without VectorE still costs 3.6 us in the old order, how much of VectorE's 6 us there is load and how much is place, and what pairing is worth in the old order.
